# One engine fewer in a conditional: the routing's fallback counts on VectorE, the search for the routing runs at another pace, and seven weight fetches move

## The chip, the cores and the metric

The kernel runs on one core of one Trainium2 chip. The metric is the device time of one execution in microseconds. Three runs of the kernel before gave 842.13, 843.80 and 843.88 us, so the median is 843.8 us. Times inside the program are from one profiled execution, counted from its first instruction.

The engines are called by their names in the profile: PE (TensorE's matmuls), PEld (its weight loads, which run beside the matmuls), DVE (VectorE), ACT (ScalarE), POOL (GpSimd) and SP (SyncE, which here issues nearly all transfers).

## The reference

Three layers follow each other. Inputs are float32; 2176 tokens of 512 values run through them.

```
x = attention(q, k, v)                  # windows of 32 keys either side, and 32 global tokens
x = silu(x @ w_in) @ w_out              # 512 -> 2048 -> 512
logits = x @ w_gate                     # 8 experts
order = argsort(-logits.flatten())      # best (token, expert) pair first
for token, e in order:                  # an expert takes cap = 2176 / 8 = 272 tokens
    if token is free and counts[e] < cap: assigned[token] = e
out[assigned == e] = relu(x[assigned == e] @ w1[e]) @ w2[e]
```

The greedy assignment is what the change is about: each token goes to its best expert that is not full yet, the tokens with the largest logits first.

## The kernel before, in words

The program has three stretches. First come attention and the first dense layer. Then comes the second dense layer with the routing woven into it (about 375 to 617 us). At the end stand the eight experts. The second stretch is the one that the change touches.

**The second layer.** `ORDER` holds 68 steps: 17 tiles of 128 tokens, with 4 steps to a tile. A step is 12 matmuls of 128x512 on PE (L1104), so there are 816 of them; below they are counted 0 to 815, and a tile is 48. At the head of step n stand `g_load(n + 5)` (a 256 KB load of `ht`), `g_split(n + 3)`, and, in some steps, `part` and `fetch`. `g_split` takes `ht` through SiLU (L679) and a rounding copy `ghi` (L55), both on ACT, and a difference `glo` on POOL (L58). At the end of a tile ACT copies the sum out of PSUM (L1120), and SP stores it to DRAM in `x2_d`.

**The expert weights.** `fetch(k)` (L1052) makes SP load a chunk of 512 KB into one of four buffers `eraw`. `part(k)` (L1059) splits it: ACT writes the rounded half of `we` (L55), and DVE the difference (L58). Chunks 0 to 3 are fetched at steps 38 to 44. `part(0)` to `part(6)` stand at steps 45, 47, ..., 57, each with `fetch(k + 4)` right behind it, in the same step (L1095 to L1097). That fetch writes the buffer which this very `part` reads.

**The routing** is a Python generator. `spend(0.216)` is called after each of the 816 matmuls. It subtracts 0.216 from a budget, and when the budget is used up the generator runs to its next `yield`, whose number is the new budget. So a `yield w` puts the next piece of the routing behind w / 0.216 matmuls, rounded up. Nothing else sets the place: each engine works through its instructions in the order in which the program is written.

The routing fills the experts one after the other. Seven rounds (E - 1) have three levels each. In a level, DVE compares each token's best logit with 64 values (`cmp`, L949); after `yield 4.0` in a round's first level, or 3.5 in the others, PE counts per expert with 17 small matmuls (L954); DVE marks the values at which an expert has too many (`fl`, L956); after `yield 0.9` PE adds these up on all partitions (L960). DVE then narrows the range (`z`, `zs`, `hi`, L962 to L967). After a round's third level it also takes the full expert out and picks each token's next best (`sel`, `pn`, `pl`, `Lw`, `m`, `fo`, L969 to L934). Then comes the next round's first `cmp`.

**The branch.** After the last round, `Ab` says who has which token. PE counts it once more (`total`, L939), DVE writes `badi` (L985), which is zero if every expert has 272 tokens, and a conditional block (L988 to L995) with an exact search stands behind a test of `badi`. PE and DVE both load `badi` into a register and branch, since `count` (L788) has a matmul in it. With the inputs measured, the block is skipped. Then PE counts for the slots (`pf` L1000 and `tt` L1002), a chain on DVE makes the table of slots (`sc` L1005 to `val` L1035), PE multiplies it out (L1039), and DVE makes the indices by which POOL gathers the first rows of `x2_d` (L1084).

Of the kernel before, what the change touches and what calls it, by code (L numbers as in the profile page):

```python
# [8 lines left out]
F32 = mybir.dt.float32  # L9
F32R = mybir.dt.float32r  # L10
BF = mybir.dt.bfloat16
I32 = mybir.dt.int32
AF = mybir.ActivationFunctionType
OP = mybir.AluOpType
# [13 lines left out]
def tile_kernel(ctx, tc, q_l, k_l, v_l, q_g, k_g, v_g, w_in, w_out, w_gate, w1, w2, out):  # L28
# [14 lines left out]
    # ------------------------------------------------------------------ phase 1  # L43
# [18 lines left out]
    def convert(raw, pool, shape, b=1):  # L62
        """float64 values, given as their bits, rounded to float32"""
        low, top = raw[..., 0], raw[..., 1]
        u = pool.tile(shape, I32, name="cvu", bufs=3 * b)
        v = pool.tile(shape, I32, name="cvv", bufs=b)
        nc.vector.tensor_scalar(u, top, 3, 0x3FFFFFF8, op0=OP.logical_shift_left, op1=OP.bitwise_and)
        # the low word in units of the last place, rounded
        nc.scalar.activation(v, low.bitcast(mybir.dt.uint32), AF.Copy, scale=2.0 ** -29)
        nc.vector.scalar_tensor_tensor(u, top, -0x40000000, u, op0=OP.bitwise_and, op1=OP.bitwise_or)  # L70
        nc.gpsimd.tensor_tensor(u, u, v, op=OP.add)  # L71
        m = pool.tile(shape, F32, name="cvm", bufs=b)
        nc.scalar.activation(m, top.bitcast(F32), AF.Square)
        yield None
        # what float32 has no exponent for is zero
        nc.vector.scalar_tensor_tensor(u.bitcast(F32), m, 2.0 ** -30, u.bitcast(F32), op0=OP.is_ge, op1=OP.mult)
        yield u.bitcast(F32)

    def w_in_chunk(f):
        """chunk f of the columns of w_in, as exact high and low parts"""  # L80
        k = 2 if wide else 1
        # the values as they come lie where their parts will
        raw = wp.tile([128, 512 * k], I32 if wide else F32, name=f"w{f}", bufs=1)
        src = w_in.bitcast(I32) if wide else w_in
        nc.sync.dma_start(raw.rearrange("p (c x) -> p c x", c=4),
                          src[:, k * 128 * f:k * 128 * (f + 1)].rearrange("(c p) f -> p c f", p=128))
        yield
        if wide:
            for s in convert(raw.rearrange("p (c f t) -> p c f t", c=4, t=2), ap, [128, 4, 128]):
                yield  # L90
        else:
            s = ap.tile([128, 4, 128], F32, name="cvu", bufs=3)
            nc.vector.tensor_copy(s, raw.rearrange("p (c f) -> p c f", c=4))
        t = wp.tile([128, 2, 4, 128], F32R, name=f"w{f}", bufs=1)
        nc.scalar.copy(t[:, 0], s)
        yield
        nc.gpsimd.tensor_tensor(t[:, 1], s, t[:, 0].bitcast(F32), op=OP.subtract)
        W[f] = t

    class Line:  # L100
        """chunks of w_in under way"""
# [40 lines left out]
    # ---- attention  # L142
# [31 lines left out]
    def load_n(b, c):  # L174
        """the local values as they stand, for the global queries"""
        if c == 0:
            RAW["vn", b] = ap.tile([128, 4, H, DH], F32, name="vn", bufs=1)
        nc.sync.dma_start(RAW["vn", b][:, c], v_l[b, :, 128 * c:128 * c + 128].rearrange("h p d -> p h d"))
# [3 lines left out]
    def load_v(b, qb):  # L182
        """the values under each window of keys"""
        V = VB[qb % 2]
        vn = RAW["vn", b]
        if qb == 0:
            nc.gpsimd.memset(V[0:32, 0], 0.0)
        else:
            nc.sync.dma_start(V[0:32, 0], vn[96:128, qb - 1])
        nc.sync.dma_start(V[32:96, 0], vn[0:64, qb])  # L190
        nc.sync.dma_start(V[0:96, 1], vn[0:96, qb])
        nc.sync.dma_start(V[0:96, 2], vn[32:128, qb])
        nc.sync.dma_start(V[0:64, 3], vn[64:128, qb])
        if qb == 3:
            nc.gpsimd.memset(V[64:96, 3], 0.0)
        else:
            nc.sync.dma_start(V[64:96, 3], vn[0:32, qb + 1])
        if qb < 2:
            nc.sync.dma_start(V[96:128].rearrange("p c h d -> p c (h d)"),
                              RAW["gv", b].rearrange("p h d -> p (h d)")[:, None].to_broadcast([32, 4, H * DH]))  # L200
        Vt[b, qb] = V
        if qb == 3:
            free["vn"] += 0.5
# [34 lines left out]
    def windows(b, qb, hh):  # L238
        """the keys that each 32 queries see: 96 local ones, and the global ones"""
        kw = ap.tile([128, 2, 4, 128], F32, name="kw", bufs=2)  # L240
        k = Kt[b]
        w = bass.AP(tensor=k.tensor, offset=k[:, 2 * hh, 128 * qb:].offset, ap=[k.ap[0], [576, 2], [32, 4], [1, 96]])
        nc.vector.tensor_copy(kw[:, :, :, 0:96], w)
        nc.vector.tensor_copy(kw[:, :, :, 96:128], Gt[b][:, 2 * hh:2 * hh + 2, 1].unsqueeze(2).to_broadcast([128, 2, 4, 32]))
        Kw[b, qb, hh] = kw
# [116 lines left out]
    # one tick = one new step, and one further stage of each block under way  # L362
# [67 lines left out]
    def tick(t):  # L430
# [21 lines left out]
        # the exponentials of the new block come after what the others wait for  # L452
# [8 lines left out]
    def ticks():  # L461
        for t in TICKS:
            # room for what the block leaves behind
            while t[0] == "L" and through[0] < 2 and 4 * t[1] + t[2] >= 8 + 3 * through[0]:
                yield "wait"
            yield from tick(t)
        while live:
            yield from advance()

    # ---- first layer of the dense block  # L470
# [10 lines left out]
    def unit_dram(u):  # L481
        """pre-activations, kept in DRAM"""
# [66 lines left out]
    # ---- the last three units, a chunk of the hidden layer at a time  # L549
# [6 lines left out]
    # row 32 c + e: one at column e  # L556
# [17 lines left out]
    def o_load(n):  # L574
        """row chunk n of w_out"""
        RW[n] = cv.tile([128, 512, 2 if wide else 1], I32 if wide else F32, name="wraw", bufs=4)
        src = w_out.bitcast(I32) if wide else w_out
        nc.sync.dma_start(RW[n].rearrange("p f t -> p (f t)"), src[128 * n:128 * n + 128])
# [17 lines left out]
    def o_gate(n):  # L596
        """w_out @ w_gate, in four parts and with the experts on the partitions"""
# [28 lines left out]
    # what is done to w_out after which of the groups of products  # L626
# [23 lines left out]
    # ------------------------------------------------------------------ phase 2: the second layer, and beside it the routing  # L650
# [8 lines left out]
    def gate_sum(pl, t0, nt):  # L659
        """the parts of the logits, summed and with the tokens on the partitions"""  # L660
# [89 lines left out]
    # the first slots are gathered before the last tile is done, and what it has of them is added on the chip  # L750
# [8 lines left out]
    def tables():  # L759
# [3 lines left out]
        # row of the token in the result, column j and partition p: the order of the tokens  # L763
# [24 lines left out]
    def count(sel, oh, name):  # L788
        """how many selected tokens each expert has, on every partition"""
# [4 lines left out]
        cb = t("cb", [128, E], BF)  # L794
        V_.tensor_copy(cb, c)
        ps = rs.tile([128, E], F32, name="cnt")
        nc.tensor.matmul(ps, ones, cb, start=True, stop=True)
        return ps
# [18 lines left out]
    def phase():  # L817
# [12 lines left out]
        # the largest value at which some expert has too many  # L830
# [37 lines left out]
        # among the tokens at that value: how many of them, in order  # L868
# [27 lines left out]
    def routing():  # L896
        yield from gates()
        tables()
        # ---- the experts fill up one after the other. Where the next one is full is looked for on grids of values, each
        # finer than the one before; whether the result is the exact one shows in the counts.  # L900
# [45 lines left out]
        for _ in range(E - 1):  # L946
            for l in range(3):
# [3 lines left out]
                yield 3.5 + (0 if l else 0.5)  # L951
# [5 lines left out]
                yield 0.9  # L957
                # as many values as some expert has too many tokens at
# [11 lines left out]
            # the expert that is full there  # L970
# [15 lines left out]
        yield 2.2  # L986
        rv = nc.values_load(badi[0:1, 0:1], engines=(mybir.EngineType.PE, mybir.EngineType.DVE), min_val=0, max_val=1)
# [9 lines left out]
        # ---- slots: 272 of them for each expert  # L997
        yield 0.5
# [45 lines left out]
        # which of the first 384 slots the tokens of the last tile have  # L1044
        V_.tensor_scalar(last_to, ior, slot[:, ORDER[-1][0]:ORDER[-1][0] + 1], None, op0=OP.is_equal)

    # the experts' weights come in chunks of a quarter of a layer: the first layer's columns, the second layer's rows
# [17 lines left out]
    # ---- the two together  # L1065
# [22 lines left out]
    for n, (j, q) in enumerate(ORDER):  # L1088
# [6 lines left out]
        if n in range(45, 45 + 14, 2):  # L1095
            part((n - 45) // 2)
            fetch((n - 45) // 2 + 4)  # L1097
# [3 lines left out]
        for f in range(4 * q, 4 * q + 4):  # L1101
# [4 lines left out]
            # every other tile is written by now  # L1106
# [22 lines left out]
    # ------------------------------------------------------------------ experts  # L1129
# [52 lines left out]
    # the last expert's slots, with the slots on the partitions  # L1182
# [18 lines left out]
    # expert, first slot and number of slots  # L1201
# [104 lines left out]
```

## Time and profile before

| | |
|---|---|
| median of three runs | 843.8 us |
| span of the profiled execution, first to last instruction | 838.5 us |
| median less span | 5.3 us |
| PE busy | 799.7 us, 95% of the span |
| DVE busy | 455.9 us, 54% |
| ACT busy | 393.4 us, 47% |
| POOL busy | 228.9 us, 27% |

The profiled execution's own time is its span of 838.5 us and what lies around it; no total was recorded for it apart, so the 5.3 us between the span and the median stand for what lies around it. An engine's busy time is the union of its instructions. "Idle before, releaser" says how long an engine waited in front of an instruction and which instruction let it go on. PEclk is the share of TensorE's full clock that was granted in a stretch.

### The profile page before, as it was taken

What the parts mean: (1) busy time and instruction counts of PE and PEld (TensorE: products, weight loads), DVE (VectorE), ACT (ScalarE), POOL (GpSimd) and SP (SyncE); (2) the same over time, 40 slices, a digit from 0 to 9 for tenths busy, and PEclk for the clock granted to TensorE, in tenths of its full rate; (3) what the DMA queues carried; (4) which work ended last, traced back from release to release, by engine and by line L of the source; (5) the groups of instructions that cost most, each with busy time, mean ns of one, the idle gap of its engine ahead of it and who ended that gap; (6) DMA issues with size and microseconds to landing.
All of it is one profiled execution on the core that took longest, in us unless ns stands there. A gap on an engine that the chain in (4) does not pass through costs nothing. (4 is left out here: it accounts for less than half of the span.)

```text
span 838.5 us, 18331 instructions
## 1 busy us (share of the span) xinstructions
PE 799.7 (95%) x7407; PEld 673.8 (80%) x7407; DVE 455.9 (54%) x1007; ACT 393.4 (47%) x879; POOL 228.9 (27%) x211
## 2 busy tenths in 40 slices
PE   5796899999999999999999999999799999999997
PEld 4565788788888899986667777777589999999994
DVE  4999954564555376620003544566635666666650
ACT  3676644353444467635543333454324545544531
POOL 3365400000000056634325353333230211122001
PEclk9699899999999999999999999999999999999999
DMA  9996753872772263107652334554135657566511
GB/s 221 243 258 187 174 140 95 208 186 80 181 184 79 87 204 127 44 27 227 200 165 75 90 99 126 191 174 164 60 94 163 211 179 219 196 216 211 186 63 42
DMA packets 127529, 127.35 MB, mean 152 GB/s; under 512 B 58672, under 2 KB 94528, under 8 KB 127440
## 3 DMA queue, kind: packets, MB, share of 16 engines
q1 hardware_dynamic: 124656, 117.20, 48.5%
q0 software_dynamic: 2784, 8.93, 3.0%
q8 instruction: 60, 0.98, 0.5%
q14 instruction: 29, 0.24, 0.1%
HBM read 91.24 MB, written 20.71 MB: 134 GB/s over the span
## 5 line engine op out<-in xcount | busy, mean ns | idle before, releaser
L1104 PE MATMUL acc<-w,ghi 128*128 128x512 f32 x544 | 178.9, 404 | 3.3 <-PEq L988 3.3
L477 PE MATMUL S<-xhi,w 128*128 128x384 f32 (+1 forms) x512 | 167.8, 360 | 5.0 <-ACT P L331 2.6
L1104 PEld LDWEIGHTS acc<-w,ghi 128*128 128x128 f32 x544 | 100.8, 189 | 31.3 <-issue 10.9
L1104 PE MATMUL acc<-w,glo 128*128 128x512 f32 x272 | 109.3, 402 | 0.0
L477 PEld LDWEIGHTS S<-xhi,w 128*128 128x128 f32 x512 | 96.5, 193 | 15.8 <-issue 4.7
L1214 PE MATMUL h<-xshi,we 128*128 128x272 f32 x512 | 108.7, 292 | 0.0
L58 DVE TENSOR_TENSOR we<-eraw,we 128x1024 fp32r<-128x1024 f32 x64 | 79.8, 1247 | 28.3 <-ACT we L55 28.3
L1232 PE MATMUL acc<-hh,we 128*128 128x272 f32 x448 | 93.4, 288 | 0.0
L58 POOL TENSOR_TENSOR glo<-ht,ghi 128x512 fp32r<-128x512 f32 x44 | 61.0, 1400 | 94.1 <-ACT ghi L55 89.8
L1214 PEld LDWEIGHTS h<-xshi,we 128*128 128x128 f32 x512 | 84.3, 188 | 0.1
L477 PE MATMUL S<-xlo,w 128*128 128x384 f32 (+1 forms) x256 | 83.8, 327 | 0.1
L1214 PE MATMUL h<-xslo,we 128*128 128x272 f32 x256 | 73.9, 289 | 0.0
L1232 PEld LDWEIGHTS acc<-hh,we 128*128 128x128 f32 x448 | 73.7, 188 | 0.0
L477 PE MATMUL h<-xhi,w 128*128 128x384 f32 x256 | 69.7, 341 | 0.7 <-DVE fold L558 0.7
L1218 ACT ACTIVATE hh<-h 128x272 fp32r<-128x272 f32 x64 | 25.5, 399 | 88.0 <-PE h L1214 87.3
L55 ACT CAST we<-eraw 128x1024 fp32r<-128x1024 f32 x64 | 66.8, 1043 | 0.0
L1232 PE MATMUL acc<-hl,we 128*128 128x272 f32 x224 | 64.5, 288 | 0.0
L1104 PEld LDWEIGHTS acc<-w,glo 128*128 128x128 f32 x272 | 51.5, 189 | 14.3 <-issue 2.8
L71 POOL TENSOR_TENSOR cvu<-cvu,cvv 128x512 int32<-128x512 int32 x32 | 43.5, 1359 | 66.0 <-DVE cvu L70 42.4
L1171 POOL DMA_INDIRECT out_dram<-orow,idx x17 | 17.6, 1037 | 157.6 <-DVE orow L1179 140.5
L1120 ACT COPY x<-acc 128x512 f32<-128x512 f32 x17 | 10.0, 587 | 88.2 <-PE acc L1104 87.4
L1219 DVE SCALAR_TENSOR_TENSOR hl<-h,hh 128x272 fp32r<-128x272 f32 x64 | 28.2, 441 | 41.9 <-ACT hh L1218 41.6
(229 smaller groups left out, 1504.3 us busy)
## 6 DMA issues: line engine op xcount, KB each, us to landing
eraw<-in_moe_w_dram SPq DMA_DIRECT2D x64, 512.0 KB, 3.8
ht<-h_d SPq DMA_DIRECT2D x44, 256.0 KB, 3.6
h_d<-hs SPq DMA_DIRECT2D x24, 384.0 KB, 2.8
gh<-h_d SPq DMA_DIRECT2D x12, 768.0 KB, 4.4
w<-in_moe_w_in_dram SPq DMA_DIRECT2D x16, 512.0 KB, 6.3
wraw<-in_moe_w_out_dram SPq DMA_DIRECT2D x16, 512.0 KB, 3.9
V<-vn SPq DMA_DIRECT2D x32, 192.0 KB, 3.6
x_d<-x SPq DMA_DIRECT2D x17, 256.0 KB, 2.0
```

What stands on the lines that cost most here:

```text
L55: nc.scalar.copy(hi, src)
L58: eng_lo.tensor_tensor(lo, src, hi.bitcast(F32), op=OP.subtract)
L71: nc.gpsimd.tensor_tensor(u, u, v, op=OP.add)
L477: nc.tensor.matmul(ps[:, :n], a, x[:, cc, :n], start=k == 0, stop=k == 11)
L1104: nc.tensor.matmul(ps, a[:, f % 4], x, start=f == 0 and k == 0, stop=f == 15 and k == 2)
L1120: nc.scalar.copy(x2, ps)
L1171: nc.gpsimd.indirect_dma_start(out=out, out_offset=bass.IndirectOffsetOnAxis(ap=at, axis=0), in_=r[:n], in_offset=None)
L1214: nc.tensor.matmul(ps, a, XS[e][x][:, c, o], start=k == 0, stop=k == 11)
L1218: nc.scalar.activation(hh, ps, AF.Relu)
L1219: nc.vector.scalar_tensor_tensor(hl, ps, 0.0, hh.bitcast(F32), op0=OP.max, op1=OP.subtract)
L1232: nc.tensor.matmul(ACC[i][d], a, x, start=f == 0 and k == 0, stop=f == 7 and k == 2)
```

## The change

`count`, which is called only inside the conditional block, no longer uses PE. It adds over the partitions on DVE with two 32x32 transposes and some copies. So only DVE loads `badi` and branches, and the `yield 2.2` ahead of the load is gone. Behind the block, `yield 0.5` becomes `yield 6`. In the search 3.5 becomes 3.0 (with 0.5 more in a first level, as before), and 0.9 becomes 0.8. The fetches of chunks 4 to 10 stand four steps later, at steps 49, 51, ..., 61. Comments are gone too; the core of the diff:

```
     def count(sel, oh, name):
...
-        cb = t("cb", [128, E], BF)
-        V_.tensor_copy(cb, c)
-        ps = rs.tile([128, E], F32, name="cnt")
-        nc.tensor.matmul(ps, ones, cb, start=True, stop=True)
-        return ps
+        cw = t("cw", [128, 32])
+        V_.memset(cw, 0.0)
+        V_.tensor_copy(cw[:, 0:E], c)
+        ct = t("ct", [128, 32])
+        V_.transpose(ct, cw)
+        cr = t("cr", [128, 1])
+        V_.tensor_reduce(cr, ct, axis=AX.X, op=OP.add)
+        cq = t("cq", [32, 4])
+        for g in range(4):
+            V_.tensor_copy(cq[:, g:g + 1], cr[32 * g:32 * g + 32])
...
+        return out
...
-                yield 3.5 + (0 if l else 0.5)
+                yield 3.0 + (0 if l else 0.5)
...
-                yield 0.9
+                yield 0.8
...
-        yield 2.2
-        rv = nc.values_load(badi[0:1, 0:1], engines=(mybir.EngineType.PE, mybir.EngineType.DVE), min_val=0, max_val=1)
+        rv = nc.values_load(badi[0:1, 0:1], engines=(mybir.EngineType.DVE,), min_val=0, max_val=1)
...
-        yield 0.5
+        yield 6
...
         if n in range(45, 45 + 14, 2):
             part((n - 45) // 2)
-            fetch((n - 45) // 2 + 4)
+        if n in range(49, 49 + 14, 2):
+            fetch((n - 49) // 2 + 4)
```

The numbers of matmuls between the pieces follow from the yields. From L960 to the next L954 there were 19 in a first level and 17 in the others, and there are now 17 and 14. From L954 to L960 there were 5, and there are 4. From `total` to `pf` there were 14 with the branch behind the eleventh, and there are 28. From `pf` to L1039 there are 47, as before. So the last L960 stands behind matmul 646 of the 816 (723 before), `total` behind 657 (734), `pf` behind 685 (748) and L1039 behind 732 (795).

On PE, at the branch, before (the conditional block, 716 rows of `count`'s matmuls, stands where the line is left out):

```order
L1104 MATMUL acc<-w_4879,glo 128x512
L1104 MATMUL acc<-w_4916,ghi 128x512
L987 TENSOR_LOAD badi
L987 ISA x2
L988 COMPARE_AND_BRANCH
...
L988 UNCONDITIONAL_BRANCH x2
L1104 MATMUL acc<-w_4916,ghi 128x512
```

On PE at the same place, now:

```order
L955 MATMUL cnt<-Ab,ones 128x136
L1121 MATMUL acc<-w_5083,ghi 128x512 x2
L1121 MATMUL acc<-w_5083,glo 128x512
L1121 MATMUL acc<-w_5140,ghi 128x512 x2
L1121 MATMUL acc<-w_5140,glo 128x512
L1121 MATMUL acc<-w_5189,ghi 128x512
L1003 UNCONDITIONAL_BRANCH
L1121 MATMUL acc<-w_5189,ghi 128x512
```

The load of `badi`, the test and the block are gone from PE; what is left is a jump to the rows that follow it, as ACT, POOL and SP had one before too.

On DVE, from the skipped block on, before (`sc` is the first tile of the table of slots):

```order
L988 UNCONDITIONAL_BRANCH x2
L1005 MEMSET sc 128x1 x8
L1006 COPY sc<-cnt 128x128
L1010 COPY sc<-sc 128x8
L1011 TENSOR_TENSOR sc<-sc 128x128
```

On DVE at the same place, now (`we` is the difference of a chunk of expert weights, here of `part(5)` and `part(6)`):

```order
L1003 UNCONDITIONAL_BRANCH x2
L58 TENSOR_TENSOR we<-eraw,we 128x1024 x2
L1020 MEMSET sc 128x1 x8
L1021 COPY sc<-cnt 128x128
L1025 COPY sc<-sc 128x8
```

Since the search ends 77 matmuls earlier and the `part`s stay at their steps, two of them now stand between the branch and the table of slots. They were in the search before.

On DVE, at the sixth and last change of round in the search, now (from `fl` of a third level to `cmp` of the next round's first):

```order
L972 TENSOR_SCALAR fl<-cnt 64x8
L58 TENSOR_TENSOR we<-eraw,we 128x1024
L978 TENSOR_REDUCE z<-cnt 128x1
L980 TENSOR_SCALAR zs<-z,step 128x1
L983 TENSOR_TENSOR hi<-hi,zs 128x1
L985 TENSOR_SCALAR sel<-m,hi,zs 128x17
L988 TENSOR_SCALAR pn<-cnt,z 128x8
L990 TENSOR_TENSOR pl<-sel,pn 128x136
L991 TENSOR_TENSOR Lw<-Lw,pl 128x136
L948 TENSOR_REDUCE m<-Lw 128x17
L950 TENSOR_TENSOR fo<-Lw,m 128x136
L965 SCALAR_TENSOR_TENSOR cmp<-m,hi,grid 128x17x64
```

At the same change of round before, the difference of a weight chunk stood behind the `cmp` and not ahead of `z`.

## Rows read from the trace of the kernel before

**Rows 1.** The page: the span, and busy time of each engine.

```profile
span 838.5 us, 18331 instructions
PE 799.7 (95%) x7407; PEld 673.8 (80%) x7407; DVE 455.9 (54%) x1007; ACT 393.4 (47%) x879; POOL 228.9 (27%) x211
```

**Rows 2.** Waits of PE: line waited for, us in total, times, longest.

```profile
PE acc L1104 <- PEq L988: 3.3, 1, 3.3
PE cnt L954 <- DVE cmp L949: 0.8, 2, 0.6
PE acc L1136 <- DMA xrow<-x_d,idx: 0.4, 2, 0.2
```

**Rows 3.** The branch line L988: duration in ns; who waited for it.

```profile
L988 PEldq COMPARE_BRANCH  x1: 3511/3511/3511, 595.0 to 595.0; - x1
...
  DVE sc L1005: 4.0, 1
```

**Rows 4.** The stretch 600 to 604 us: busy by engine, PEclk, DMA.

```profile
600.00:604.00 4.00, 4.00 (x12) 3.12 (x11) 3.62 (x21) 0.00 (x0) 0.00 (x0) 0.57 0.02 6
```

**Rows 5.** Timeline of PE, the search: start us, us, line, tile.

```profile
491.71 0.18 PE L960 MATMUL cnt<-fl,ones 64*128 64x8 bf16 x1
496.37 0.70 PE L954 MATMUL cnt<-fo,cmp 128*64 128x8 bf16 x17
498.37 0.18 PE L960 MATMUL cnt<-fl,ones 64*128 64x8 bf16 x1
502.57 0.70 PE L954 MATMUL cnt<-fo,cmp 128*64 128x8 bf16 x17
516.10 0.70 PE L954 MATMUL cnt<-fo,cmp 128*64 128x8 bf16 x17 [0.60 <-DVE cmp L949]
556.89 0.16 PE L960 MATMUL cnt<-fl,ones 64*128 64x8 bf16 x1 [0.23 <-DVE fl L956]
```

**Rows 6.** Timeline of DVE, two changes of round (first row, then the others).

```profile
494.12 1.35 DVE L949 SCALAR_TENSOR_TENSOR cmp<-m,hi,grid 128x1088 bf16<-128x1088 f32 x1
...
511.43 0.92 DVE L967 TENSOR_TENSOR hi<-hi,zs 128x1 f32<-128x1 f32 x1
513.72 1.07 DVE L934 TENSOR_TENSOR fo<-Lw,m 128x136 bf16<-128x136 f32 x1
514.71 1.34 DVE L949 SCALAR_TENSOR_TENSOR cmp<-m,hi,grid 128x1088 bf16<-128x1088 f32 x1
```

**Rows 7.** Lines of DVE: duration ns least/median/most over the program.

```profile
L967 DVE TENSOR_TENSOR hi<-hi,zs x21: 158/160/1187, 460.7 to 589.0; 128x1 f32<-128x1 f32 x21
L1029 DVE TENSOR_SCALAR cmp<-ior,df x17: 279/281/289, 603.8 to 607.0; 128x128 bf16<-128x128 f32 x17
L1035 DVE TENSOR_TENSOR val<-hi,df x2: 464/1006/1547, 607.7 to 608.0; 128x289 bf16<-128x289 f32 x2
```

**Rows 8.** Timeline of POOL, the differences glo.

```profile
511.04 1.29 POOL L58 TENSOR_TENSOR glo<-ht,ghi 128x512 fp32r<-128x512 f32 x1 [0.93 <-POOL glo L58]
...
548.35 2.55 POOL L58 TENSOR_TENSOR glo<-ht,ghi 128x512 fp32r<-128x512 f32 x2 [5.75 <-ACT ghi L55]
551.85 1.29 POOL L58 TENSOR_TENSOR glo<-ht,ghi 128x512 fp32r<-128x512 f32 x1 [0.95 <-ACT ghi L55]
```

**Rows 9.** Timeline of ACT from the end of a tile.

```profile
546.45 0.59 ACT L1120 COPY x<-acc 128x512 f32<-128x512 f32 x1 [4.43 <-PE acc L1104]
...
549.31 1.04 ACT L55 CAST we<-eraw 128x1024 fp32r<-128x1024 f32 x1
```

**Rows 10.** Timeline of PE, from the last count to the table of slots.

```profile
592.68 0.22 PE L939 MATMUL cnt<-Ab,ones 128*128 128x136 bf16 x1 [1.45 <-DVE Ab L978]
...
599.49 0.23 PE L1000 MATMUL cnt<-Ab,upper 128*128 128x136 bf16 x1
...
611.98 0.59 PE L1039 MATMUL cnt<-val,cmp 128*128 128x34 bf16 x17
```

**Rows 11.** Timeline of DVE, where the table of slots begins.

```profile
599.82 0.29 DVE L1006 COPY sc<-cnt 128x128 f32<-128x128 f32 x1 [1.68 <-PE cnt L1002]
```

More of the change, by code (lines that the diff above doesn't have):

```diff
@@ L793, in count @@
         V_.tensor_reduce(c, pr.rearrange("p j e -> p e j"), axis=AX.X, op=OP.add)
-        cb = t("cb", [128, E], BF)
-        V_.tensor_copy(cb, c)
-        ps = rs.tile([128, E], F32, name="cnt")
-        nc.tensor.matmul(ps, ones, cb, start=True, stop=True)
-        return ps
+        cw = t("cw", [128, 32])
[8 more added lines that the diff above has]
+            V_.tensor_copy(cq[:, g:g + 1], cr[32 * g:32 * g + 32])
+        cs = t("cs", [32, 1])
+        V_.tensor_reduce(cs, cq, axis=AX.X, op=OP.add)
+        cb = t("cb", [32, 32])
+        V_.tensor_copy(cb, cs.to_broadcast([32, 32]))
+        ca = t("ca", [32, 32])
+        V_.transpose(ca, cb)
+        out = t("co", [128, E])
+        for g in range(4):
+            V_.tensor_copy(out[32 * g:32 * g + 32], ca[:, 0:E])
+        return out
     def over(sel, oh):
```

## The prediction

> **What bounds the kernel now.** I read the page first: PE is busy for 799.7 of 838.5 us [rows 1], so a change is worth what it takes from PE's waits or adds to them. The waits of PE come next. In the second layer they are few: 3.3 us at the branch, 0.8 us for `cmp` in two waits, and 0.4 us for the first gathered rows after the layer [rows 2]; the timeline adds 1.45 us before the last count [rows 10] and 0.23 us for one `fl` [rows 5]. Everything else is matmuls back to back. So the bound is PE's own stream, and the routing costs time only where PE comes to one of its pieces before DVE has made it. The timelines of DVE, POOL and ACT then show how early DVE is, place by place.
>
> **What goes.** The branch stood in PE's stream for 3.5 us [rows 3], and PE lost 3.3 us by it [rows 2]. After this wait the clock was halved: PEclk is 0.57 in the stretch from 600 to 604 us [rows 4], so 4.0 x 0.43 = 1.7 us went there. The wait for the gather, 0.4 us [rows 2], goes as well: the indices are made 63 matmuls earlier, and the gathers are issued in the last tile as soon as the routing is over. Together 5.4 us. The Trainium skill (Runtime: NRT & Kernel Launch, Instruction fetch mechanics) has it that a taken branch breaks the sequential prefetch and waits for its target's page. The rows agree, and by that rule the size of the skipped block does not matter, so DVE should still wait about as long as it did.
>
> DVE does keep its branch. From the last count at 592.68 [rows 10] to the table's first row on DVE, 5.2 us went by: the start of that wait of 4.0 us [rows 3] is the end of `badi`, about 1.1 us after the count. PE now passes 28 matmuls between the two, and a matmul takes 0.23 us (4.66 us with 19 of them against 4.20 us with 17, from the first four of [rows 5]). That is 6.4 us, so DVE's branch is hidden with 1.2 us to spare. If that cover is gone, each us beyond costs one.
>
> **The search's new pace.** A change of round now has 4.66 - 2 x 0.23 = 4.20 us from L960 to L954 instead of 4.66. The other levels have 4.20 - 3 x 0.23 = 3.5 us. What does DVE need? At the third change, `cmp` ended at 494.12 + 1.35 = 495.47, which is 3.76 us after L960 at 491.71 [rows 5, 6]. That is free running. At the fourth it needed more: `hi` took 0.92 us where the median is 0.16, and `fo` took 1.07 [rows 6, 7]. The difference on POOL that ran from 511.04 to 512.33 [rows 8] ends within 0.02 us of `hi`. So these DVE instructions wait while POOL subtracts. `cmp` ended at 516.05, and PE waited 0.60 us [rows 5]. So a change of round needs 3.8 us alone and 4.8 to 5.3 us with POOL at work; the levels between need 2.2 us alone, and with a wait of 1 us still fit into 3.5.
>
> Where does POOL work? The end of a tile sets it. ACT copies the sum out at 546.45 [rows 9]; POOL's first two differences run from 1.9 to 4.45 us later, the next begins 5.4 us later [rows 8]. Those offsets I carry to the new order of matmuls, with the tile's end as zero, 0.85 us for the 17 small matmuls and 0.23 for a large one:
>
> - Fifth change (L960 after matmul 532, tile end at 528). L960 runs at 1.8. `hi` is due at 2.4 and waits for POOL's first difference, to 3.3; `pl` waits for the second, to 4.7; `cmp` ends at about 7.2. PE comes at 1.8 + 4.2 = 6.0. It waits 1.2 to 1.6.
> - Sixth change (L960 after 589, tile end at 576). L960 runs at 3.8, but DVE has `we` of `part(2)` ahead of `z`. ACT's half of it ends 3.9 us after the tile's end (549.31 + 1.04 - 546.45, [rows 9]), and DVE then waits for POOL and subtracts, to 5.6. The round's 3.55 us from `z` on and one more meeting with POOL (1.1) end at 10.3. PE comes at 8.0 and waits 2.3. Without POOL it would be 0.8.
> - The other four changes meet POOL on one side only and fit. The first `cmp` ends when it ended before, and PE comes 2 matmuls earlier than the 266th: 0.4 us.
>
> That is 1.4 + 2.3 + 0.4 = 4.1, in place of 0.8: plus 3.3 us. From below: no meetings, 0.4 + 0.8 - 0.8 = plus 0.4. From above: all six changes at 5.3, so 6 x 1.1 + 0.8 = plus 6.6. I take the middle, since the first of these offsets was 1.9 us in nine of ten tiles (one row stands for them). `fl` has 4 matmuls instead of 5, and the one that already came late behind a `we` [rows 5] costs about 0.3 us more. Before the last count DVE's work and PE's eleven matmuls are as they were: 1.3 us for 1.45, minus 0.1.
>
> **The table of slots.** From `pf` at 599.49 to L1039 at 611.98 PE had 47 matmuls [rows 10], 1.7 us of it lost to the clock. At full clock these are 47 x 0.23 = 10.8 us. DVE's chain ran from 599.82 [rows 11] to 608.0 + 1.55 = 609.6, of which 1.1 us is one meeting with POOL (1547 ns against 464, [rows 7]): 8.7 us alone. Then it began 0.33 us after `pf`; now `we` of `part(6)` stands ahead of it. `pf` runs 3.0 us after the end of a tile (matmul 672), ACT's half of that chunk ends at 3.9, POOL's pair at 4.45, so DVE begins the chain at about 5.2 and ends at 13.9 alone. PE comes at 3.0 + 10.8 = 13.8. Before, POOL had one difference to make beside this chain, since only the last tile was left; now it has the second pair of one tile and the first pair of the next. With two to two and a half meetings at 1.1 us, PE waits 2.7. Bounds: 0 (none) and 4.5 (four).
>
> Here the Trainium skill (SBUF — State Buffer, Who interferes with whom) speaks against the change even more. It says that VectorE and GpSimd share one port pair under an exclusive lock, for instructions with two SBUF inputs, and for copies and `tensor_scalar` in a 2-port mode. By it the 17 comparisons of this chain could wait too, which the trace cannot show, as POOL was idle beside them. They took 281 ns for 128 elements [rows 7]; if they wait as the others do, a rival follows, below.
>
> **The clock again.** A wait of 3.3 us was followed by a halved stretch, the wait of 1.45 us ahead of it alone was not. The new waits of 2.3 and 2.7 us lie between. I count one such loss for the two of them, 1.7 us; bounds 0 and 3.4.
>
> **The fetches.** They stood behind the `part` that empties their buffer, so SP waited there with the `ht` loads behind it. Four steps later the buffer is long free, and SP runs on. PE never waited for `ghi` or `glo`, so this gains nothing by itself. Chunk k now has 48 matmuls, 11 us, until its `part`; it loses nothing either, unless landing took three times as long as in the rest of the layer.
>
> **Sum.** -5.4 + 3.3 + 0.3 - 0.1 + 2.7 + 1.7 = plus 2.5 us. The profiled span goes from 838.5 to 841.0. The median lies 5.3 us above that span, and I keep this: 843.8 + 2.5 = 846.3 us. Less than 0.2%, 1.7 us, can't be told from no change here.
>
> **Rivals.**
>
> 1. POOL is out of step and DVE meets it hardly anywhere. Then the old waits for DVE go as well (0.8 + 0.2 + 1.45), and what comes is 0.4 + 0.8 + 0.1. Sum: -5.4 - 2.5 + 1.3 = -6.6, 837.2 us. For it: four of the six old changes paid nothing. Against it: POOL's offset to a tile's end hardly varies. With half of the meetings it is about 841.5. Chance 0.20 for all cases below 842.1.
> 2. The meetings come as forecast but shorter, or the clock holds: 843.8 + 2.5 - 1.7 - 1 = 843.6, no change. Chance 0.23.
> 3. The 17 comparisons lock too, or both long waits halve the clock: plus 1.3 to 2.6, or plus 1.7, so 848 to 849 us. Chance 0.10.
> 4. The change does not free PE: the jump that is left in its stream costs it a fetch like the branch did, or DVE's branch outlasts 28 matmuls. Up to 3.3 us more, 849.6. Against it: ACT, POOL and SP had such a jump before, and no wait on the page names it. Chance 0.05.
>
> The forecast itself, 845.5 to 848, has 0.42. Cases of both signs hold much of the chance; the forecast's own range is 844.5 to 848. Faster: 0.20. Same: 0.23. Slower: 0.42 + 0.10 + 0.05 = 0.57. The range for 8 in 10 runs from 840.5 (half the meetings, cut at 0.1 below) to 849.5.
>
> **What would show it.** In the profile after: no PE wait at the branch and PEclk 1.0 behind it; PE waiting for `cmp` over 3 us in total, most of it at the last two changes of round; a wait of 2 to 3 us at the table's matmul (L1054 there), with `we` just ahead of `sc` on DVE; `pf` not waiting. No such wait at the table would make the forecast wrong by its largest single term, and waits for `cmp` that stay under 1 us by the next. A PE wait at `pf` would speak for the fourth rival.

## The result, and the profile after

Five runs of the changed kernel gave 850.59 to 855.11 us, median 852.66; five of the kernel before beside them 842.13 to 846.48, median 843.88. The ratio is 1.0095 [1.0068, 1.0123]. The change makes the kernel slower by 8.8 us. Forecast were 846.3, with 840.5 to 849.5 as the range: the sign was right, the size was not.

The profiled execution of after is the slowest of its five (855.11 us, span 853.4), and the one of before had a shorter span than any timed run explains: in the later profiles time less span is 1.7 to 2.0 us, so 838.5 answers to some 840.3, and no run of before was under 841.77. One part of that spread has nothing to do with the change. From the start to the first of the 816 matmuls the programs do the same work, and nine profiles of nine kernels give 374.8 us (before, the least) to 379.3 for it (after: 379.0; the pace alone, whose program is that of before up to there: 378.2). So the stages are compared, not the spans:

| us, from one profile each | before | after | difference |
|---|---|---|---|
| start to the first matmul of the second layer | 374.8 | 379.0 | +4.2, not the change |
| first to last of the 816 matmuls | 242.3 | 253.9 | +11.6 |
| last of them to the end | 221.4 | 220.45 | -1.0 |

The last stage takes 220.4 us in seven of the nine profiles. The two others, before and the old pace below, are those in which PE waits for gathered rows.

The page after, against [rows 1]:

```profile
span 853.4 us, 18320 instructions
PE 800.4 (94%) x7407; PEld 675.0 (79%) x7407; DVE 461.1 (54%) x1007; ACT 393.7 (46%) x879; POOL 228.0 (27%) x211
```

PE does the same 7407 matmuls; the time went into its waits and its clock. The waits answer to [rows 2] (line waited for, us in total, times, longest):

```profile
PE cnt L970 <- DVE cmp L965: 6.4, 5, 2.8
PE cnt L1054 <- DVE val L1050: 6.3, 1, 6.3
PE cnt L955 <- DVE Ab L994: 0.9, 1, 0.9
```

The waits at the branch and for the gathered rows are gone from the list, as meant. In their place PE waits 6.4 us for `cmp` and 6.3 us at the table of slots. In the second layer that is 13.6 us, against 3.3 + 0.8 + 1.45 + 0.23 = 5.8 before [rows 2, 5, 10]: +7.8 of the +11.6. The other 3.8 us go with the clock. Less PE's waits, the layer takes 234.4 to 234.6 us in the three later profiles in which PEclk stays at 1.00 all through it (the old pace, POOL without reads, another pace), 236.6 before and 240.3 here (busy PE, then PEclk, against [rows 4]):

```profile
core 0: us, PE busy (x), PEclk, DMA share, GB/s
548.00:552.00 4.00, 4.00 (x24) 0.50 0.00 0
552.00:554.00 2.00, 2.00 (x6) 0.50 0.00 0
...
572.00:574.00 2.00, 2.00 (x6) 0.50 0.00 0
574.00:576.00 2.00, 2.00 (x8) 0.80 0.00 0
...
610.00:612.00 2.00, 0.03 (x1) 0.50 0.01 2
612.00:614.00 2.00, 2.00 (x21) 0.50 0.00 0
```

Three times PE runs at the lower of its two levels (1.2 GHz), and each time it had stood just before. Before the change it happened once. The three long waits on PE's timeline:

```profile
547.97 1.07 PE L970 MATMUL cnt<-fo,cmp 128*64 128x8 bf16 x17 [2.45 <-DVE cmp L965]
570.09 0.70 PE L970 MATMUL cnt<-fo,cmp 128*64 128x8 bf16 x17 [2.79 <-DVE cmp L965]
611.97 0.66 PE L1054 MATMUL cnt<-val,cmp 128*128 128x34 bf16 x17 [6.26 <-DVE val L1050]
```

These are the fifth and the sixth change of round, and the table. Why is DVE late? First the fifth change, on DVE and POOL, against [rows 6, 8]:

```profile
541.49 2.56 POOL L58 TENSOR_TENSOR glo<-ht,ghi 128x512 fp32r<-128x512 f32 x2 [5.89 <-PE cnt L976]
545.23 1.27 POOL L58 TENSOR_TENSOR glo<-ht,ghi 128x512 fp32r<-128x512 f32 x1 [1.18 <-ACT ghi L55]
```

```profile
541.91 0.89 DVE L983 TENSOR_TENSOR hi<-hi,zs 128x1 f32<-128x1 f32 x1
542.73 1.35 DVE L985 TENSOR_SCALAR sel<-m,hi,zs 128x17 f32<-128x17 f32 x1
...
545.24 1.41 DVE L950 TENSOR_TENSOR fo<-Lw,m 128x136 bf16<-128x136 f32 x1
```

POOL's first two differences end at 542.8 and 544.05, the third at 546.5; `hi`, `sel` and `fo` end within 0.15 us of these. `hi` takes 0.16 us alone, `sel` 0.29, `fo` 0.30, so the three meetings cost 0.7 + 1.1 + 1.1 = 2.9 us. Then the table, against [rows 3, 7, 8, 11]; first POOL, then DVE:

```profile
593.82 7.14 POOL L58 TENSOR_TENSOR glo<-ht,ghi 128x512 fp32r<-128x512 f32 x4 [6.74 <-ACT ghi L55]
604.92 2.51 POOL L58 TENSOR_TENSOR glo<-ht,ghi 128x512 fp32r<-128x512 f32 x2 [3.96 <-ACT ghi L55]
608.74 1.27 POOL L58 TENSOR_TENSOR glo<-ht,ghi 128x512 fp32r<-128x512 f32 x1 [1.31 <-issue]
```

```profile
593.85 4.59 DVE L58 TENSOR_TENSOR we<-eraw,we 128x1024 fp32r<-128x1024 f32 x2 [4.51 <-DVEq L1003]
598.38 0.11 DVE L1020 MEMSET sc<- 128x1 f32 x7
...
598.68 0.94 DVE L1025 COPY sc<-sc 128x8 f32<-128x8 f32 x1
...
599.85 1.15 DVE L1025 COPY sc<-sc 128x16 f32<-128x16 f32 x1
...
604.18 6.49 DVE L1044 TENSOR_SCALAR cmp<-ior,df 128x128 bf16<-128x128 f32 x17
...
611.08 0.83 DVE L1050 TENSOR_TENSOR val<-hi,df 128x289 bf16<-128x289 f32 x2
```

DVE leaves its branch at 593.85, just as POOL begins four differences in a row. The two `we` take 2.3 us each (1.2 where POOL rests), two small copies 0.94 and 1.15 us (0.2 alone), and the 17 comparisons 6.49 us where they had run from 603.83 on before, in 3.42 us. One line of a view by source shows what happened to them (least, median, most ns):

```profile
L1044 DVE TENSOR_SCALAR cmp<-ior,df x17: 272/277/1319, 604.2 to 610.4; 128x128 bf16<-128x128 f32 x17
```

Three of them took 1.3 us each, one beside each of POOL's three differences from 604.92 on; the others ran as before [rows 7]. PE came to `pf` at 594.67 and waited for nothing there:

```profile
594.67 0.23 PE L1015 MATMUL cnt<-Ab,upper 128*128 128x136 bf16 x1
```

So the branch is off PE's path, with 0.8 us to spare, but DVE stands at it for 4.5 us (4.0 before, [rows 3]), and the two `we` that wait behind it now come ahead of the table.

### The profile page after: what moved, and what is told of

Its sections match the earlier page's. It is cut to its first block, busy times and chain, and to the rows that moved or that the text cites. A ratio compares the mean times of both kernels' runs of the same rounds, so it can differ in the third digit from the quotient of the medians.

```text
span 853.4 us, 18320 instructions
## 1 busy us (share of the span) xinstructions
PE 800.4 (94%) x7407; PEld 675.0 (79%) x7407; DVE 461.1 (54%) x1007; ACT 393.7 (46%) x879; POOL 228.0 (27%) x211
## 5 line engine op out<-in xcount | busy, mean ns | idle before, releaser
L1121 PE MATMUL acc<-w,ghi 128*128 128x512 f32 x544 | 184.3, 412 | 0.0
```

What stands on the lines that cost most here:

```text
L1121: nc.tensor.matmul(ps, a[:, f % 4], x, start=f == 0 and k == 0, stop=f == 15 and k == 2)
```

## The experiments

Theory: every loss is PE waiting for DVE, which POOL's reads hold up, and the lower clock that follows PE's longer waits. Rivals: the moved fetches; PE's leftover jump; DVE's own work or its branch, without POOL. All runs were timed in five rounds beside the kernel before; the first four beside a median of 844.03 us, the last three beside 843.85.

**The old pace.** The changed kernel with the two numbers of the search as they were.

```
-                yield 3.0 + (0 if l else 0.5)
+                yield 3.5 + (0 if l else 0.5)
...
-                yield 0.8
+                yield 0.9
```

> The changed kernel with the old pace of the search (3.5 and 0.9), so the branch on VectorE alone and the later fetches are tried without the faster search. Theory (VectorE is late where it meets GpSimd's differences, and PE's waits then halve the clock): waits for cmp fall from 6.4 to about 1 us, no difference of a weight chunk stands ahead of the table of slots, and beside that chain GpSimd has one difference left, so the wait of 6.3 us at the table is 0 to 1 us. The routing ends 14 large matmuls later than before, so PE waits about 3 us for the gathered rows behind the layer. Sum against before: -5.0 + 3 = about 842 us (840.5 to 844.5). Rival (the later fetches or the larger block cost the time): 848 us or more, with the search's waits as small as before.

Measured: 840.55 us, ratio 0.9957 [0.9938, 0.9976]. As expected: freeing PE of the branch gains when the search has its time. PE's two longest waits of the layer and what follows it:

```profile
PE acc L1153 <- issue: 2.8, 1, 2.8
...
PE cnt L955 <- DVE Ab L994: 1.5, 1, 1.5
```

The layer is 237.7 us, 4.6 less than before; the predicted 3.3 + 1.7 for branch and clock is of that size. But the stage behind it is 226.3 us, 4.9 more: the table now ends where the layer does, POOL issues the gathers at 616.6 to 619.2, and the first rows land after PE's last matmul at 617.0. PE stands 2.8 us there ("issue": the view names no releaser), and the clock falls in that wait: PEclk is 0.50 from 620 to 626 us. So this profile, the slowest of the run's ten executions (845.01 us), gives the gain back there; the medians are still 3.5 us apart.

**The pace alone.** The kernel before, with 3.0 for 3.5 and 0.8 for 0.9; branch, table and fetches as they were.

> The kernel before with the faster search alone (3.0 and 0.8); PE keeps its branch, the fetches stay. Theory: PE waits 4 to 6 us more for cmp, most of it at the last two changes of round, 2 to 4 us more at the table of slots, still 3.3 us at the branch, and loses 3 to 5 us more to the clock: 852 to 860 us. Rival (the loss comes from the branch's new form or from the fetches): within 2 us of 844.

Measured: 848.61 us, ratio 1.0056 [1.0038, 1.0073]. Slower, but by less than I expected (852 to 860), and outside the rival's range too. The waits for `cmp` come as in after (5.3 us in five), the branch keeps its 3.8, but the table costs 0.6 instead of 6.3:

```profile
PE cnt L954 <- DVE cmp L949: 5.3, 5, 2.8
PE acc L1104 <- PEq L988: 3.8, 1, 3.8
...
PE cnt L1039 <- DVE val L1035: 0.6, 1, 0.6
```

The reason is one of place. Here `pf` stands behind matmul 671, and `part(6)` at 684 comes behind the chain (its `we` runs at 606.10, after `val`); in after `pf` stands behind 685, and both `we` are ahead of the chain. The chain began 0.5 us after `pf` here. PE also took 12.4 us from `pf` to the table, 1.4 more than in after, since the halved stretch behind its branch lies there. So the pace by itself explains the waits for `cmp` and not the table.

**POOL without reads.** The changed kernel with `glo` set to zero by POOL; the low half of the second layer's left operand is left out. ACT, DVE and all places stay.

```
-        split(hi, lo, g, nc.scalar, nc.gpsimd)
+        nc.scalar.copy(hi, g)
+        nc.gpsimd.memset(lo.bitcast(F32), 0.0)
```

> The changed kernel in which GpSimd fills the low half of the second layer's left operand with zeros instead of subtracting (that half is left out of the result; everything else is computed). Theory (GpSimd's reads hold VectorE up): what stays of the waits is 0.4 us at the first cmp, up to 0.8 at the last change of round and under 0.5 at the table; no halved clock in the second half of the layer; 836 to 840 us. Rival (VectorE's own work is too long for the new pace, whatever GpSimd does): waits of more than 4 us stay, 846 us or more.

Measured: 835.19 us, ratio 0.99 [0.9883, 0.9918], 17.5 us under the changed kernel. That is 0.8 us below the range I gave. The two waits that made it slow all but vanish, and the second layer has no stretch at the lower clock:

```profile
PE cnt L1055 <- DVE val L1051: 1.0, 1, 1.0
PE cnt L971 <- DVE cmp L966: 0.7, 1, 0.7
```

DVE has the same instructions, the same branch and the same two `we` ahead of the table. So neither they nor PE's jump alone make it late. The comparisons fall to 3.7 us in all, least/median/most 269/281/716 ns.

This run takes away the reads and more than half of POOL's time at once: a fill takes 0.53 us, a difference 1.27. Rows of DVE beside a fill tell the two apart in part. `we`, `pl` and `val`, which read two tiles, ran in their usual time there (1.23, 0.30 and 0.46 us). A small copy took 0.45 us instead of 0.18, and two comparisons 0.72 and 0.59 instead of 0.28: these waited for the fill too, but for a fill's time. So what reads two tiles was held by POOL's reads; for the copies and comparisons the run shows only that POOL's shorter work holds them less.

**The fetches back.** The changed kernel with each fetch in the step of its `part` again.

> The changed kernel with the fetches of chunks 4 to 10 back in the steps of their parts. Theory: the fetches are beside the point, 851 to 854 us, with the waits for cmp and for the table within 1.5 us of the changed kernel's 6.4 and 6.3. Rival (the later fetches let the loads of ht and so GpSimd's differences run into VectorE's pieces): the waits halve, 847 us or less.

Measured: 852.08 us, ratio 1.0089 [1.0069, 1.0108], and waits of 6.4 and 6.1 us at the same places. The moved fetches neither cost nor gain anything that shows.

Two things differ from the profile of after although the waits do not. The wait at the table has other parts: here `we` began just before POOL (591.11 and 591.20), the two took 1.2 and 1.3 us, and the comparisons took 8.6, so only the sum of the meetings is steady and not where they fall. And the halved stretch at the fifth change lasts 3.4 us where after's lasts 6.8, and the layer is 252.7 us, 1.2 less. So some of after's +11.6 belongs to that one execution.

**The table later.** The changed kernel with 28 matmuls more between `pf` and the table's matmul.

```
-        yield 10
+        yield 16
```

> The changed kernel with `yield 16` for `yield 10` ahead of the table of slots, so that PE multiplies it out behind matmul 760 instead of 732; nothing else. Theory (VectorE is late with the table by 6.3 us, since two `we` and the chain meet GpSimd's reads, and PE's clock falls behind that wait): 28 matmuls more, 6.4 us, so PE waits 0.3 to 0.9 us at the table, the halved stretch of 6.8 us behind it is gone (3.4 us), and all falls by 8 to 9.5 us, less what comes back at the gather (0 to 1 us): 843 to 846 us. The waits for `cmp` stay at 5 to 6.5 us. Rival (the table is late because its chain runs behind the conditional of VectorE wherever it stands, or the wait moves to the gather): the time stays at 850 to 853 us.

Measured: 843.81 us, ratio 1.0003 [0.9986, 1.002], 8.9 us less than after. The layer is 244.6 us; the wait at the table is 0.8, and nothing comes back at the gather:

```profile
PE cnt L970 <- DVE cmp L965: 5.2, 5, 2.7
...
PE cnt L1054 <- DVE val L1050: 0.8, 1, 0.8
```

With this one place mended the excess over before is gone, and what the branch gave pays for the waits for `cmp`. DVE's comparisons took 7.6 us here, with POOL beside them for longer, and the 28 matmuls covered all but 0.8 us of the lateness. At the fifth change PE waited 1.32 us from 542.84 to 544.16 here, and the clock still fell behind it:

```profile
core 0: us, PE busy (x), PEclk, DMA share, GB/s
542.00:544.00 2.00, 0.84 (x4) 1.00 0.93 351
544.00:546.00 2.00, 1.83 (x21) 0.95 0.05 18
546.00:548.00 2.00, 1.59 (x6) 0.50 0.00 0
```

**The parts later.** The changed kernel with the two `we` behind the table.

```
-        if n in range(45, 45 + 14, 2):
-            part((n - 45) // 2)
+        if n in (45, 47, 49, 51, 53, 62, 64):
+            part((45, 47, 49, 51, 53, 62, 64).index(n))
...
-        if n in range(49, 49 + 14, 2):
-            fetch((n - 49) // 2 + 4)
+        if n in (49, 51, 53, 55, 57, 66, 67):
+            fetch((49, 51, 53, 55, 57, 66, 67).index(n) + 4)
```

> The changed kernel with `part(5)` and `part(6)` moved from steps 55 and 57 to 62 and 64, behind the table's matmul, and `fetch(9)` and `fetch(10)`, which write their buffers, to steps 66 and 67; this takes the two `we` away that stand ahead of the table's chain on VectorE and leaves GpSimd's reads as they are. Theory (of the 6.3 us at the table the two `we`, 2.3 us each behind GpSimd's reads, are one half, and meetings inside the chain the other): PE waits 2.5 to 4 us at the table, the halving behind it is shorter or gone, 847 to 851 us. If the reads of GpSimd that held the `we` now hold the chain instead, the wait stays near 5 us and the time at 850 to 853. Rival (the `we` alone make the table late, and GpSimd does not matter): the wait falls to under 1 us, 843 to 846 us.

Measured: 846.85 us, ratio 1.004 [1.0022, 1.0059]. The wait at the table is 2.6 us, within the theory's 2.5 to 4; the time is 0.15 us under its range. What is left of the wait is POOL inside the chain (DVE, then POOL):

```profile
594.31 1.23 DVE L1030 TENSOR_TENSOR sc<-sc,Ab 128x136 f32<-128x136 f32 x1
...
597.43 3.42 DVE L1044 TENSOR_SCALAR cmp<-ior,df 128x128 bf16<-128x128 f32 x17
...
601.26 2.85 DVE L1050 TENSOR_TENSOR val<-hi,df 128x289 bf16<-128x289 f32 x2
```

```profile
594.09 2.60 POOL L58 TENSOR_TENSOR glo<-ht,ghi 128x512 fp32r<-128x512 f32 x2 [1.86 <-ACT ghi L55]
600.80 3.00 POOL L58 TENSOR_TENSOR glo<-ht,ghi 128x512 fp32r<-128x512 f32 x2 [4.11 <-ACT ghi L55]
```

`val` takes 2.85 us for two instructions of 0.46, while the comparisons, which fall between POOL's pairs, run free in 3.4 us. So without the two `we` ahead of it the wait is 3.7 us shorter: the chain begins 0.3 us after `pf` instead of 3.7. It still takes 13.2 us, since its meetings with POOL have only moved, and they make the rest.

**Another pace.** The changed kernel with the time put where DVE was late: the last `total`, `pf` and the table stand behind matmuls 712, 737 and 789.

```
-                yield 3.0 + (0 if l else 0.5)
+                yield 3.0 + (0 if l else 1.5)
...
-                yield 0.8
+                yield 0.9
...
-        yield 2.2
+        yield 3.6
...
-        yield 6
+        yield 5.3
...
-        yield 10
+        yield 11.2
```

> The changed kernel with the yields set by where VectorE was late: 1.5 more instead of 0.5 in the first level of a round (4.5), 0.9 at `fl`, 3.6 ahead of the last count, 5.3 at `pf`, 11.2 at the table; no branch on PE. Places: last count behind matmul 712, `pf` 737, table 789. Theory (every loss was PE waiting for VectorE and the clock behind it, so giving VectorE the time at these places gets the branch's 3.3 us and the clock's 1.7 us back): waits for `cmp` 0 to 1.5 us, none over 1 us at the table, at the gather or at the old branch, no halved stretch in the second layer, 836 to 839 us. Rival (part of the loss of the changed kernel is not a wait, as in more work on VectorE or a jump on PE): 842 us and above.

Measured: 835.08 us, ratio 0.9894 [0.9875, 0.9913], 8.8 us under before and faster than both kernels. The layer is 236.8 us:

```profile
PE cnt L970 <- DVE cmp L965: 1.8, 3, 0.6
PE cnt L976 <- DVE fl L972: 0.4, 2, 0.2
```

```profile
core 0: us, PE busy (x), PEclk, DMA share, GB/s
520.00:560.00 40.00, 39.76 (x266) 1.00 0.50 165
560.00:600.00 40.00, 39.11 (x225) 1.00 0.50 159
600.00:614.00 14.00, 14.00 (x78) 1.00 0.24 68
```

Nothing waits at the old branch, at the table or at the gather, and PEclk is 1.00. The `cmp` waits are 0.3 us above what I allowed them and the time 0.9 us under what I expected. The rival, that PE loses something that is no wait, falls: its jump and DVE's longer block are still in this kernel.

## Why the prediction was wrong

**The branch and the gather, -5.4: right.** No wait is left at either place, and the clock holds behind the branch. The old pace shows the layer 4.6 us shorter. The fourth rival (a jump on PE, DVE's branch too long) falls: `pf` waits for nothing, and DVE is 0.8 us early where I had 1.2. DVE's own wait at the branch is 4.5 us for 4.0. By the Trainium skill (Runtime: NRT & Kernel Launch, Instruction fetch mechanics) a taken branch waits for the page of its target where that lies outside the window already fetched; the trace comes near to that, since the wait hardly grew with the longer block.

**The search, +3.3: right in kind, too small.** The places were right: waits of 0.3 at the first `cmp` (0.4 forecast), 2.45 at the fifth change (1.2 to 1.6) and 2.79 at the sixth (2.3); to these come 0.5 at the second (495.84 us; the prediction calls this one the third), which I had let fit, and 0.4 later. The 0.3 that I had added for `fl` did not come: no wait for `fl` is left, where before had one of 0.23. POOL kept its offset to the tile's end: ACT's copy at 539.59, POOL's first difference 1.9 us later. The fifth failed on the count of meetings: I let `hi` and `pl` wait, but `hi`, `sel` and `fo` did. I took `sel`, a `tensor_scalar`, for immune, since in before its seven rows were all near 0.29 us. They had only never met POOL but in its last 0.06 us.

**The table, +2.7: this term failed most.** It cost 6.3 us and lay outside my bounds (0 to 4.5). PE came as forecast, 605.7 - 594.67 = 11.0 us after `pf` (10.8). DVE began the chain 598.38 - 594.67 = 3.7 us after `pf`, where I had 2.2, and needed 611.9 - 598.4 = 13.5 us for it, where I had 8.7 and two to two and a half meetings, 11.2. The first is 1.5 us: I had one `we` ahead of the chain, timed by ACT. The order shown ahead of the prediction has two, and both stand behind the branch, which DVE leaves only at 593.85. I had asked whether the branch ends before PE comes to `pf`, and not what queues behind it. The second is 2.3 us: there were five meetings (two copies, 0.75 + 0.95 us more than alone, and three comparisons, 1.0 each), 4.7 us. Together 3.8, for the 3.6 that are missing. This split is that of one profile: with the fetches back, the chain began 2.6 us after `pf` and took 14.5, for a wait of 6.1.

**The 17 comparisons.** Three of them took about 1.3 us. I had put this aside as a rival of 0.10. The Trainium skill (SBUF — State Buffer, Who interferes with whom) counts `tensor_scalar` and copies among the instructions that can contend for the shared port pair. Here the trace agrees: 272/277/1319 ns beside GpSimd's reads, 279/281/289 without [rows 7]. That no such wait was seen before was no evidence, since POOL was idle beside these rows.

**The clock, +1.7: too small.** I counted one stretch for two waits, and three came, 6.8, 3.4 and 6.8 us long. Waits grew from 5.8 to 13.6 us, and 253.9 - 242.3 - 7.8 leaves 3.8 us more for the clock than before, where the sum had no net change (-1.7 + 1.7). I had taken one stretch as the likeliest and two as a rival, on a single pair of rows, 3.3 us and 1.45 us; the fifth change I had left out.

**The fetches, 0: right; PE's last count, -0.1: small and right in sign.** The first by the run with the fetches back (852.08 against 852.66); the count waits 0.9 for 1.45, so 0.5 less.

**The sum.** In the layer I had +2.9 of waits and no clock; measured were +7.8 and +3.8. Of the 8.7 us between, 3.6 are the table, 1.3 the rest of PE's waits and 3.8 the clock. The stage in front makes the profile dearer still by 4.2 us that the median does not show: the stages of the layer and behind it give 11.6 - 1.0 = 10.6 us in the profiles, the medians 8.8. Of the 1.8 between, 1.2 may be the longer stretch at the fifth change in after's profile, as the run with the fetches back suggests; the rest is open. Keeping 5.3 us between median and span misread one profile with a short start, but it cancels in 843.8 + 2.5 and is no part of the miss.

**The range.** The two large terms go the same way, since a wait that grows by POOL also brings the clock. I gave their upper ends 0.10 between them, as if only one could come; the table's upper bound and two stretches of clock together would have been 846.3 + 1.8 + 1.7 = 849.8, and still not 852.7.

## What to carry to other kernels

When an engine is freed from a wait, look at the engine that still has it: what queues behind it there, and who meets it when it runs off late. Rows without a delay show nothing about contention unless the other engine was at work beside them. Where one stream is paced by hand, give each piece the time that its partner needs at its worst place, for a wait there can be paid twice, in itself and in the clock that falls with it.

## What the runs showed of the hardware

- Beside GpSimd's `tensor_tensor` of 128x512 (1.27 us), VectorE's instructions of several forms lasted until it ended, however small they were: one element per partition (`hi`, 158 to 1098 ns), 17 (`sel`, 284 to 1354), 128 (comparisons, 272 to 1319), and 1024 (`we`, 1.2 to 2.3 us). Not all forms did: `zs`, a `tensor_scalar` of one element, took 212 to 215 ns in all its 21 rows of after, ten of them beside POOL's work, and a `tensor_reduce` (`slot`) 298 ns within such a difference in the run with the pace alone.
- The wait goes both ways, and what began first ran through. In after POOL began 0.03 us ahead of `we`, and `we` took 2.34 us; with the table later `we` began 0.11 us ahead of POOL and took 1.23, and POOL's difference took 2.29.
- Beside GpSimd's fills (0.53 us), `tensor_tensor`s of two tiles ran as alone, and copies, casts and comparisons did not (POOL without reads).
- The granted clock fell to its lower level in or behind waits of 2.45, 2.79 and 6.3 us (after), 3.3 (before), 2.8 (the old pace) and 2.6 (the parts later), and held after 1.45 (before) and 1.5 (the old pace). With the table later it fell also behind one of 1.32 us at the fifth change. So the length of a wait alone does not decide it; what does was not tried here.
- A fall that begins during a wait costs less than one behind it, since PE stands through its first part (at the table in after, 610 to 612 us: PEclk 0.50, PE busy 0.03).
